# Fewer changes of TensorE tiling: products that take their neighbours' form, reversed keys, merged masks

## The chip, the cores and the metric

The kernel runs on one core of a Trainium2 chip. The metric is device time in microseconds (us); the kernel before takes 242.95 us, the median of three runs (242.12 to 243.84).

A core has five engines that run side by side, each with its own queue of instructions: TensorE (PE, matrix products, with a separate record PEld for the loading of weights), VectorE (DVE), ScalarE (ACT), GpSimd (POOL) and SyncE (SP), which here only issues DMA transfers. They wait for one another through semaphores. TensorE writes to PSUM, eight banks of 512 float32 columns in 128 partitions; VectorE and ScalarE read PSUM and write SBUF; GpSimd works within SBUF.

## The reference, cut to what matters

Two branches over the same 2048 tokens of width 640 are mixed by a gate. Branch A is attention in four segments of 512 tokens, 32 heads of width 20, causal within a segment, with a memory carried from segment to segment. Branch B is a Fourier filter over tokens and width.

```python
def _A_ref(x, wq, wk, wv, wo, beta):
    ...                                   # q, k, v: [B, 32, 4, 512, 20]
    phi = lambda t: jnp.where(t > 0, t + 1.0, jnp.exp(t))
    mask = (ar[:, None] < ar[None, :]) * -1000000000.0
    g = _sigmoid(beta)
    for s in range(4):
        logits = einsum('bhqd,bhkd->bhqk', qs, ks) * scale + mask
        a_dot = einsum('bhqk,bhkd->bhqd', softmax(logits), vs)
        a_mem = einsum('bhld,bhde->bhle', phi(qs), M) / (einsum('bhld,bhd->bhl', phi(qs), z) + 1e-06)
        outs.append(g * a_mem + (1.0 - g) * a_dot)
        M = M + einsum('bhld,bhle->bhde', phi(ks), vs)
        z = z + einsum('bhld->bhd', phi(ks))
    return o @ wo

def _B_ref(x, w_r, w_i):
    X = rfft2(x.astype(float32)) * (w_r + 1j * w_i)
    return irfft2(X, s=(S, D)).astype(bfloat16)

g = _sigmoid((x * gate_w).sum(-1, keepdims=True))
return g * a + (1 - g) * b
```

## The kernel before, in words

The kernel does not issue instructions by hand. `record` lists every operation with its engine (or two engines that may take it), the buffers that it reads and writes, and a priority; `Sched.op` derives from the buffers which operations must come before which. `Sched.schedule` then takes a long list of numbers, `ORDER`, which fixes the sequence of every engine's queue and, where there is a choice, the engine: each number is twice an operation's index plus the choice. `emit` writes the instructions and puts a semaphore wait ahead of an operation where what it needs is not yet known to be done. PSUM banks are handed out from two pools while the list is followed, 0 to 3 for the attention scores (`qk`) and 4 to 7 for all else (`gen`).

**Tiling of TensorE.** A product may use the whole 128x128 array or a part of it. Four forms occur. Whole-array products (mode 0: projections, the Fourier products F1, D, T, Tb, Db, the memory's read and update); products of 128 rows by 32 columns, four beside each other (mode 2: `projd`, `pvf`, `Fb`); products with 20 rows for the scores (mode 1); and 128x64 pairs (mode 4: v tiles of odd token blocks). Mode -1 leaves the form open: `mms` then writes the product either whole or as four 32-wide pieces, by what stands beside it in TensorE's queue. Before, only the output projection of the first three segments (line 513) is of mode -1. The pieces are written at line 513, everything else at line 515.

**Attention.** For each segment `project` makes q and k (five tiles of 128 rows each, five products deep), v (`v_tile`, four blocks of 128 tokens in two halves of 16 heads) and the gate's column, which is a 321st column of the second half's weights (`gw`). The keys of a segment stand in the order of `token_order`: even blocks of 128 first, then the odd blocks, with the two halves of 64 of each odd block exchanged. To match, odd v tiles are made as two products of 64 columns each that land in exchanged partitions. `qk_unit` makes the scores of a group of four heads in three kinds of unit, ScalarE takes the exponential (line 1265) into one of three slots of `ex`, GpSimd zeroes what lies above the diagonal with `affine_select` (line 1286, in `mask`), and `pv_flipped` or, for the last segment, `pv_group` multiplies by v.

**Fourier.** `fold` sums and differences the halves of x (lines 902 and 907, on VectorE or GpSimd), F1 and D transform, T applies the twiddle factors, line 1441 multiplies with the filter W out of PSUM on VectorE, line 1446 combines, Tb and Db transform back, line 1487 sums the halves into G. Copies out of PSUM are lines 524 (ScalarE) and 526 (VectorE).

**End.** `finish_tile` adds, for each 128 tokens, the gated Fourier part (`Fb`) and the output projection in one bank, copies it into `ot` and stores it.

**Queues.** All loads and stores but two go by SyncE's queue, in the list's order; line 547 is a transposing load, line 549 a plain one. At the start its order is an xsb load (x for the Fourier branch), the first transposed chunk of x, beta, the first 192 columns of wk, two transposes of two chunks each, and then the rest of wk; the first columns of wq go by ScalarE's queue. A DMA waits besides until the one that lies 1.6 MB of transfers back has landed.

## Time and profile before

| | before |
|---|---|
| median of three runs, us | 242.95 (242.12 to 243.84) |
| span of the profiled execution, us | 239.9 (the page states no other time of it) |
| TensorE busy, us | 225.7 (94%) |
| weight loads busy, us | 138.7 (58%) |
| VectorE busy, us | 195.9 (82%) |
| ScalarE busy, us | 199.1 (83%) |
| GpSimd busy, us | 165.8 (69%) |
| granted TensorE clock | 1.000 |
| exponentials, line 1265 | 138.7 us busy on ScalarE, 92 instructions |
| masks, line 1286 | 121.3 us busy on GpSimd, 224 instructions |
| odd v tiles, 128x64 products | 160 instructions |

A busy share is an average over stages with different limits. The span runs from the first to the last instruction; the device time has some 3 us besides. Matmuls are pipelined, so that the records of neighbouring products overlap and their mean length says less than the distance from one start to the next. The chain that ended last is followed backwards from the last instruction, at each step to what released it; its shares say which engine set the pace. A wait is idle time of an engine just before an instruction, put down to what came last.

### The profile page before, as it was taken

How to read it: one execution, taken by the hardware profiler on the slowest of the kernel's cores; microseconds unless marked ns; L12 is line 12 of the kernel's file. 1: busy time of each engine (PE TensorE's matmuls, PEld its weight loads, DVE VectorE, ACT ScalarE, POOL GpSimd, SP SyncE). 2: the span in 40 equal slices, each digit the busy share in tenths (PEclk: the TensorE clock that was granted, in tenths of full speed). 3: DMA queues.
4: the chain of work that ended last, by engine and by line, in shares of the span. 5: the costliest groups of instructions: out<-in, count | busy, mean ns of one | idle time of the engine just before them, and what ended most of it. 6: DMA issues, size and time to landing. Idle time of an engine off the chain costs nothing.

```text
span 239.9 us, 9221 instructions
## 1 busy us (share of the span) xinstructions
PE 225.7 (94%) x3837; PEld 138.7 (58%) x3849; DVE 195.9 (82%) x481; ACT 199.1 (83%) x241; POOL 165.8 (69%) x297
## 2 busy tenths in 40 slices
PE   7899999999999999999989999899999998998994
PEld 2475567765456566455646555455544456665793
DVE  0479998889899996898999798997988887855563
ACT  2189688898899999999999979999999987896730
POOL 8514259457969956937974999875899867686820
PEclk9999999999999999999999999999999999999999
DMA  7999869984996795473788672364766698992223
GB/s 157 270 369 234 228 177 182 311 156 112 209 263 161 128 240 170 106 240 76 239 221 251 159 222 65 103 168 138 193 193 187 202 220 127 100 110 80 61 85 109
DMA packets 58924, 42.11 MB, mean 176 GB/s; under 512 B 30020, under 2 KB 55172, under 8 KB 58884
## 3 DMA queue, kind: packets, MB, share of 16 engines
q1 hardware_dynamic: 57844, 40.96, 70.2%
q8 instruction: 30, 0.49, 0.9%
q10 hardware_dynamic: 1040, 0.57, 0.8%
q14 instruction: 10, 0.08, 0.1%
HBM read 23.32 MB, written 12.30 MB: 148 GB/s over the span
## 4 chain that ended last, share of the span: by engine, by line
PE 57%; DVE 17%; ACT 15%; DMA 4%; issue 3%; SPq 2%; POOL 0%; DVEq 0%; ACTq 0%
PE psum L515 51%; ACT ex L1265 10%; PE psum L513 6%; DVE Pt L1441 3%; DMA out_dram<-ot 2%; DMA wk<-in_A_wk_dram 2%; SPq L547 2%; DVE xsb L907 2%; DVE xf L902 2%; ACT et L1073 1%; DVE va L1116 1%; DVE ub L526 1%; DVE phk L1086 1%; DVE q L526 1%; DVE phk L1085 1%
## 5 line engine op out<-in xcount | busy, mean ns | idle before, releaser
L1265 ACT ACTIVATE ex<-psum 128x2048 bf16<-128x2048 f32 (+4 forms) x92 | 138.7, 1507 | 12.6 <-PE psum L515 11.2
L1286 POOL TENSOR_SCALAR_AFFINE_SELECT ex<-ex 128x256 bf16<-128x256 bf16 (+2 forms) x224 | 121.3, 563 | 39.0 <-ACT ex L1265 35.6
L515 PE MATMUL psum<-xT,wk 128*128 128x256 bf16 (+1 forms) x280 | 34.0, 273 | 1.0 <-DMA wk<-in_A_wk_dram 0.8
L515 PE MATMUL psum<-qkp 20*64 20x64 bf16 (+5 forms) x1024 | 31.5, 266 | 3.4 <-ACT ex L1265 2.4
L515 PE MATMUL psum<-wv,xT 128*64 128x320 bf16 (+3 forms) x240 | 30.1, 303 | 0.4 <-DVE va L1116 0.3
L515 PE MATMUL psum<-xT,wq 128*128 128x512 bf16 (+1 forms) x123 | 27.1, 380 | 0.8 <-DMA xT<-in_A_x_dram 0.5
L1441 DVE TENSOR_TENSOR Pt<-psum,Wt 128x642 bf16<-128x642 f32 x32 | 25.6, 822 | 2.3 <-PE psum L515 1.9
L515 PEld LDWEIGHTS psum<-xT,wk 128*128 128x128 bf16 (+1 forms) x280 | 19.9, 97 | 7.5 <-DMA wk<-in_A_wk_dram 1.1
L515 PEld LDWEIGHTS psum<-qkp 20*64 20x64 bf16 (+1 forms) x1024 | 12.2, 100 | 20.4 <-ACT ex L1265 14.4
L513 PE MATMUL psum<-wo,oU 128*32 128x320 bf16 x480 | 21.9, 300 | 0.0
L907 POOL TENSOR_TENSOR xsb<-xf 128x320 bf16<-128x320 bf16 (+2 forms) x12 | 9.4, 787 | 16.6 <-DVE xsb L907 12.4
L515 PEld LDWEIGHTS psum<-wv,xT 128*64 128x64 bf16 (+1 forms) x240 | 14.9, 105 | 7.7 <-issue 2.6
L1116 DVE TENSOR_TENSOR va<-psum,ebx 128x320 bf16<-128x320 f32 x32 | 15.2, 483 | 4.4 <-ACT gate L1114 2.3
L515 PE MATMUL psum<-big,Ac 128*128 128x160 bf16 (+2 forms) x96 | 18.1, 258 | 0.7 <-DVE Pt L1441 0.3
L515 PE MATMUL psum<-big,Cp 128*128 128x321 bf16 (+1 forms) x96 | 18.1, 303 | 0.2 <-DVE G L1487 0.2
L515 PE MATMUL psum<-ex,va 128*32 128x512 bf16 (+4 forms) x480 | 17.3, 275 | 0.9 <-DVE Pt L1441 0.3
L1487 DVE TENSOR_TENSOR G<-eo,psum 128x320 bf16<-128x320 f32 x32 | 14.7, 482 | 3.5 <-PE psum L515 2.5
L526 DVE CAST ot<-psum 128x320 bf16<-128x320 f32 x21 | 10.0, 490 | 8.7 <-PE psum L513 5.3
L515 PE MATMUL psum<-tt,Yt 128*128 128x256 bf16 (+1 forms) x96 | 16.5, 275 | 0.3
L515 PEld LDWEIGHTS psum<-ex,va 128*32 128x32 bf16 x480 | 10.4, 96 | 9.9 <-POOL ex L1286 3.3
L1073 ACT ACTIVATE et<-qu 128x512 bf16<-128x512 bf16 x25 | 15.6, 629 | 0.2
L513 PEld LDWEIGHTS psum<-wo,oU 128*32 128x32 bf16 x480 | 12.0, 96 | 4.6 <-issue 1.2
(99 smaller groups left out, 391.1 us busy)
## 6 DMA issues: line engine op xcount, KB each, us to landing
qkp<-qk_scr SPq DMA_DIRECT2D x28, 160.0 KB
tt<-tab_tt SPq DMA_DIRECT2D x8, 512.0 KB, 3.9
qk_scr<-qu SPq DMA_DIRECT2D x12, 256.0 KB, 3.5
u_scr<-ub SPq DMA_DIRECT2D x12, 256.0 KB, 4.0
xsb<-in_A_x_dram SPq DMA_DIRECT2D x8, 320.0 KB, 6.4
oU<-u_scr SPq DMA_DIRECT2D x15, 128.0 KB, 3.1
out_dram<-ot SPq DMA_DIRECT2D x12, 160.0 KB
Wt<-in_B_w_r_dram SPq DMA_DIRECT2D x16, 80.2 KB, 3.4
```

Of the source, the lines that this page charges most:

```text
L513: h = e.matmul(dst, wt, r_, start=st, stop=sp_, **{**kw, "tile_position": (0, q), "skip_group_check": True})
L515: h = e.matmul(o_, l_, r_, start=st, stop=sp_, **kw)
L526: alts["dve"] = (lambda e: e.tensor_copy(dst(), src()), 67 + 1.04 * n, 68.0)
L547: return e.dma_start_transpose(d_, s_)
L902: self.either(lambda e, r=r, op=op: e.tensor_tensor(xf.ap(r * 642, [321, 2], [1, 320]), xs.ap(o, [D, 2], [1, 320]), xs.ap(o + 320, [D, 2], ...
L907: self.either(lambda e, dst=dst, src=src, d0=d0, n=n, op=op: e.tensor_tensor(xs.ap(o + dst, [D, 2], [1, n]), xf.ap(src + d0, [321, 2], [1, ...
L1073: self.one("act", lambda e: e.activation(et.ap(0, [1, L]), qsl(), ACT.Exp), L, [qb], [b("et", pi_)], late, name="phi_exp")
L1116: self.one("dve", lambda e: e.tensor_tensor(va.ap(i * H * VW + h0 * VW, [VW, nh], [1, DH]), self.ps(bank, 0, [DH, nh], [1, DH]), self.ebx. ...
L1265: self.one("act", lambda e, d=d, q=q: e.activation(self.ex.ap(*d), self.ps(bank, *q), ACT.Exp, scale=SC), n, [bank], [self.exb(s, 2 * pr + ...
L1286: self.one("pool", lambda e: e.affine_select(self.ex.ap(e0 + d0, [1280, 4], [1, n], np_=np_), self.ex.ap(e0 + s0, [1280, 4], [1, n], np_=np_),
L1441: self.one("dve", lambda e, ri=ri, Pt=Pt, Wt=Wt, wo_=wo_, bank=bank: e.tensor_tensor(Pt.ap(ri * 322, [644, 2], [1, KD]), self.ps(bank, 0, ...
L1487: self.one("dve", lambda e, q=q, n2=n2, bank=bank, eo=eo: e.tensor_tensor(self.G.ap(n2 * D + 639 * q, [1 - 2 * q, 320]), eo.ap(q, [1, 320] ...
```

## The change

The change has six parts.

1. All products of mode 0 that belong to the projections, the v tiles, the Fourier branch and the memory become mode -1, so that they may run as four 32-wide pieces where a neighbour does. The 64-wide mode 4 is gone.
2. The keys of odd blocks are now in fully reversed order (step -1 over 128 tokens) in place of exchanged halves. For v, a copy `xR` holds the odd blocks of x reversed; it is made once for each segment on GpSimd or ScalarE, and odd v tiles are plain products with it. The gate's column of odd tiles comes from the unreversed x, by a product with one column.
3. With reversed keys the masks have another shape: two of three become narrower, and the masks of two neighbouring groups of heads may be one instruction (`gs`).
4. Dependencies are kept finer: the two halves of a v tile (`vb`), the two halves of the fold's buffer and its four results (`xsf`, `xs_done`), the parts of the exponentials (b0, b1, b2, c0, c1). Within one engine an order that only comes from reuse of a bank no longer costs a wait (`ordered`), and the waits ahead of one instruction are sorted by when they are expected to end.
5. Banks are no longer handed out from pools but listed (`HOMES`).
6. `ORDER` is a new list, so that every queue has another sequence and other choices of engine: for instance 24 of 32 sums of line 1446 lie on GpSimd instead of 16, and at the start SyncE issues the transposes first, while the first part of wk goes by ScalarE's queue.

```diff
@@ Sched.op
+        for b in w2:
+            if not isinstance(b, Bank):
+                dep(b.w)
+                for q in b.r:
+                    dep(q)
+        o.hard = set(preds)
         for b in w2:
-            bb = b
             if isinstance(b, Bank):
                 o.banks.append(b)
                 b.ops.append(o)
-                bb = b.buf
-            dep(bb.w)
-            for q in bb.r:
-                dep(q)
+                dep(b.buf.w)
...
+    def ordered(p, o):
+
+        return p.eng == o.eng and not p.dma and (p.eng == "pe" or p in o.preds and p.id not in o.hard)
...
@@ emit
-                if p.eng == "pe" and e == "pe":
+                if self.ordered(p, o):
                     continue
...
-                self.Sc.schedule(self.POOLS, self.ORDER)
+                self.Sc.schedule(self.ORDER, self.HOMES)
...
+        self.xR = [T(f"xR{i}", [P, 10 * P], at=(self.tt[0].off, self.tt[1].off, self.on.off, self.on.off + 2560)[i]) for i in range(4)]
...
@@ fold
-                [b("xsb", q)], [b("xf", k)], 1.0, name="fold")
+                [b("xsb", q)], [b("xf", k, r)], 1.0, name="fold")
...
-                [b("xf", k)], [b("xsb", q)], 1.0, name="fold")
+                [b("xf", k, src // 642)], [b("xsf", q, n_)], 1.0, name="fold", after=[b("xsb", q)])
+
+    def xs_done(self):
+
+        return [self.b("xsb", q) for q in range(8)] + [self.b("xsf", q, n_) for q in range(8) for n_ in range(4)]
@@ project
+        xR = self.xR[s]
+        self.Sc.group += 1
+        rev = lambda: (xR.ap(0, [256, 5], [P, 2], [1, P]), xT.ap(2 * P - 1, [L, 5], [256, 2], [-1, P]))
+        self.Sc.op({"pool": (lambda e: e.tensor_copy(*rev()), 1340.0, 50.0), "act": (lambda e: e.activation(*rev(), ACT.Copy), 1130.0, 110.0)},
+                   r=xb, w=[b("xR", s)], prio=t0, name="xrev", after=[b("xf", k, r) for k in range(3) for r in range(2)] if s > 1 else ())
@@ token_order
-        return [(0, 256, lambda: xT.ap(c * L, [256, 2], [1, P])), (256, 256, lambda: xT.ap(c * L + P + 64, [256, 2], [-64, 2], [1, 64]))]
+        return [(0, 256, lambda: xT.ap(c * L, [256, 2], [1, P])), (256, 256, lambda: xT.ap(c * L + 2 * P - 1, [256, 2], [-1, P]))]
@@ proj_tile (the same for memrd, mupd, F1, D, T, Tb, Db)
-            self.mms(items, [b("w" + which + "a"), b("w" + which + "b"), xb[c], bank], [], prio, name="proj", mode=0)
+            self.mms(items, [b("w" + which + "a"), b("w" + which + "b"), xb[c], bank], [], prio, name="proj", mode=-1)
@@ v_part
-            for p0, t0, n in ((0, 64, 64), (64, 0, 64)) if i % 2 else ((0, 0, P),):
...
-            self.mms(items, [b("wv"), xb[c], bank] + ([b("gw")] if h0 else []), [], prio, name="vproj", mode=4 * (i % 2))
+            items = [((lambda c=c: (self.ps(bank, 0, [1, w]), xR.ap(c * 256 + (i // 2) * P, [1, P]) if i % 2 else xT.ap(c * L + i * P, [1, P]),
+                                    self.wv.ap(c * (D + 1) + h0 * DH, [1, w]), c == 0, c == 4, {"skip_group_check": True})), w)]
+            if h0 and i % 2:
+                items.append(((lambda c=c: (self.ps(bank, 320, [1, 1]), xT.ap(c * L + i * P, [1, P]),
+                                            self.wv.ap(c * (D + 1) + D, [1, 1]), False, c == 4, {"skip_group_check": True})), 1))
+            self.mms(items, [b("wv"), xb[c], bank] + ([b("xR", s)] if i % 2 else []) + ([b("gw")] if h0 else []), [], prio, name="vproj", mode=-1)
...
+    def vb(self, s, lts, h0, nh):
+
+        return [self.b("va", s % 2, lt, h) for lt in lts for h in range(2) if h0 < 16 * h + 16 and h0 + nh > 16 * h]
@@ qk_unit (masks)
-                self.mask(s, g, 64, 512, 512, P, (), ("b0", "m1"), prio, -64)
+                self.mask(s, gs, 64, 576, 576, 64, (), ("b0",), prio, -63, 1)
...
-                self.mask(s, g, P, 512, 0, 64, ("a0",), ("m1",), prio, 64)
+                self.mask(s, gs, P, 512, 0, 64, ("a0",), ("m1",), prio, 1 - P, 1)
...
-                self.mask(s, g, 64, 1152, 1152, P, (), ("c0", "m3"), prio, *((0, -512) if s < 3 else (-64, 64)))
+            for gs in (gs,) if self.exo(s, gs[1]) > self.exo(s, gs[0]) else (gs[:1], gs[1:]):
...
+                self.mask(s, gs, 64, o, o, 64, (), ("c1",), prio, -63, 1)
...
@@ mask
-            self.ex.ap(e0 + d0, [1280, 4], [1, n], np_=np_), self.ex.ap(e0 + s0, [1280, 4], [1, n], np_=np_),
-            [[0, 4], [step, n // 64], [1, 64]], ALU.is_ge, 0.0, base=base, channel_multiplier=-1), 4 * n, [self.exb(s, g, k) for k in rk],
+            self.ex.ap(e0 + d0, [1280, n4], [1, n], np_=np_), self.ex.ap(e0 + s0, [1280, n4], [1, n], np_=np_),
+            [[0, n4]] + ([[64, n // 64]] if n > 64 else []) + [[1, 64]], ALU.is_ge, 0.0, base=base, channel_multiplier=cm), n4 * n,
...
@@ fft
-                         2 * P * 2048, [], [b("tt", ti)], early, name="ld_tt")
+                         2 * P * 2048, [], [b("tt", ti)], early, name="ld_tt", after=[b("xR", g // 2)] if g < 4 else ())
```

The first two copies `xR` lie where the twiddle tables `tt` come later, so the first loads of `tt` wait for the odd v tiles of the first two segments.

More of the change, by code (lines that the diff above doesn't have):

```diff
@@ L198, in schedule @@
-        while len(self.order) < len(order):
-            best = None
-            for e in self.eng:
-                t = head(e)
-                if t is not None and (best is None or t < best[0] - 1e-9):
-                    best = (t, e)
-            if best is None:
-                raise RuntimeError("order cannot be kept: " + str([(e, queue[e][pos[e]].name, queue[e][pos[e]].id) for e in self.eng if pos[e] < len(queue[e])]))
-            t, e = best
-            o = queue[e][pos[e]]
-            pos[e] += 1
-            for b in o.first:
-                _, b.pool, b.bank = place(b, level)
-                for q in range(b.bank, b.bank + b.n):
-                    level[b.pool][q] = None
-                    o.dyn.extend(users.get(q, ()))
-            o.t0 = t
+            for b in o.banks:
+                if b.ops[0] is o:
+                    for q in range(b.bank, b.bank + b.n):
+                        assert users[q] is not None
+                        t = max(t, level[q])
+                        o.dyn.extend(users[q])
+                        users[q] = None
@@ L228, in schedule @@
                 free[e] += 43.0
-                gate = window()
-                if gate is not None:
-                    o.dyn.append(gate)
+                tot, i = 0, len(issued) - 1
+                while i >= 0 and tot <= self.WINDOW:
+                    tot += issued[i].nbytes
+                    i -= 1
+                if i >= 0:
+                    o.dyn.append(issued[i])
                 issued.append(o)
@@ L1465, in fft @@
                            r=[bank], w=[b("Cp", g, c0)], prio=prio3, name="ev_Tb",
-                           after=[b("xsb", q) for q in range(8)])
+                           after=self.xs_done())
         cpb = [b("Cp", g, c0) for g in range(16) for c0 in (0, 2)]
```

190 lines of the change are left out of this document (78 added, 112 removed), and 202 rows, old and new, of tables (HOMES, ORDER).

## The prediction

> **What bounds the kernel now.** I read the page's first part, then the chain that ended last, then TensorE's waits, and last its timeline, for the price of a change of tiling.
>
> ```profile
> span 239.9 us, 9221 instructions
> PE 225.7 (94%) x3837; PEld 138.7 (58%) x3849; DVE 195.9 (82%) x481; ACT 199.1 (83%) x241; POOL 165.8 (69%) x297
> PE 57%; DVE 17%; ACT 15%; DMA 4%; issue 3%; SPq 2%; POOL 0%; DVEq 0%; ACTq 0%
> ```
>
> TensorE works 94% of the span and carries 57% of the chain. VectorE and ScalarE carry 17% and 15% of it, GpSimd nothing. In the table by stretch, with TensorE, weight load, VectorE, ScalarE and GpSimd busy in that order after the length,
>
> ```profile
> 60.00:180.00 120.00, 115.03 (x1706) 66.22 (x1715) 108.71 (x269) 113.45 (x125) 94.01 (x177) 1.00 0.68 177
> ```
>
> ScalarE stands close behind TensorE: 113.45 of 120 us. So TensorE sets the time, and ScalarE is the next to be late. The view of TensorE's own waits is short; its list sums to some 9 us, led by
>
> ```profile
> PE psum L515 <- ACT ex L1265: 2.4, 9, 0.4
> PE psum L515 <- ACT ot L524: 1.5, 2, 0.9
> PE psum L515 <- DVE G L798: 1.3, 1, 1.3
> PE psum L515 <- DMA wk<-in_A_wk_dram: 0.8, 2, 0.6
> ```
>
> Busy time hides a second loss. TensorE's timeline (start, length, then the products) shows it by its starts:
>
> ```profile
> 60.15 0.38 PE L515 MATMUL psum<-xT,wq 128*128 128x512 bf16 x1
> 60.36 0.23 PE L515 MATMUL psum<-big,Ac 128*128 128x161 bf16 x1
> 60.43 0.38 PE L515 MATMUL psum<-xT,wq 128*128 128x512 bf16 x1
> 60.74 0.73 PE L515 MATMUL psum<-ex,va 128*32 128x512 bf16 x20
> ...
> 231.01 2.40 PE L515 MATMUL psum<-wo,oTl 128*32 128x320 bf16 x64
> 233.23 0.31 PE L515 MATMUL psum<-G,fbg 128*32 128x320 bf16 x4
> ```
>
> A 512-column product is followed after 0.21 us by another whole-array one (60.15 to 60.36), but after 0.31 us by a 128x32 one (60.43 to 60.74): 0.10 us for the change of tiling. Over all such pairs of starts the middle excess over the columns is 96 ns from whole to 32 wide, 109 back, 96 from whole to the 20-row form, 106 back, 101 from the 64-wide form to whole. I count 232 changes in the old order of instructions: **23.7 us** of the span.
>
> **The change, part by part.**
>
> *Tiling.* In the new order of instructions I count 171 changes instead of 232. Per direction at the prices above this is 17.7 us, so **-6.0**. Thirty of the old changes touch the 64-wide form, which is gone; the others fall away where a product runs in its neighbour's form. They fall over the four segments of the sequence as 11, 19, 15 and 15 fewer.
> What a split costs: four 128x32 pieces stand for one whole product (TensorE instructions 3849 to 4926). The 64 pieces from 231.01 are 16 sets of 320 columns and take 2.22 us, 139 ns a set; 320 columns at the 0.21 us per 512 of a whole product are 131 ns. Over all neighbours of one form the middle is 136 ns for both. I take nothing; with 374 sets newly split and 8 ns for each, the upper end is +3.0.
> [...] The trace does not show a loss: 32-wide loads take 96 ns each, whole ones 97, and both hide. [...]
>
> *Columns.* Over the two orders, columns times their rate (1/2.4 ns, as 512 in 0.213 us) are 179.8 and 179.3 us: **-0.5**, from the products whose keys come 64 wide.
>
> *Gate column.* Odd v tiles take their operand from xR, which is reversed, so the gate's column needs its own product with one column from xT: 40, of which 5 sets are split. The nearest row is the 21-column product, 25 ns from start to start (40 in 1.0 us from 227.89 to the change before 228.98): **+1.0**. Below nothing is excluded, since work is only added; the upper end is a load each, 96 ns, +3.8.
>
> *Reversed keys.* The k projection reads its second half with step -1. No product of before has such an operand. A gain is excluded, since it reads the same elements. The lower end is 0: VectorE's fold reads one operand backwards and takes 353 ns for 320 columns, a forward sum of 321 takes 365; GpSimd's fold takes 758 against 732. The upper end is half rate: 100 whole products of 256 columns and 10 sets, 107 ns more each, +11.8. I take 0, from the rows with the same step.
>
> *The copy xR.* Four of 128x1280. Two are on ScalarE, whose 1280-element activation takes 1.24 us; two on GpSimd, between 1.1 us (its memset's 0.87 ns per element) and 2.8 (its two-input sum, 1402 ns per 640). The first stands in ScalarE's queue before the first exponential, which waited 0.93 us for TensorE at 13.7; so 0.3 us may show, and behind it wait beta's exponential and all of ScalarE. I leave it in the range. The copy on GpSimd is hidden by its 31% of idle time. Odd v tiles wait for xR; if that cover fails, the products behind one wait up to 2.8 us.
>
> *Masks.* Per row: 128 of 478 ns, 64 of 670, 32 of 691 become 126 of 478, 33 of 670 to 691, 32 of 691: 124.3 to 105 us. Not on the chain (POOL 0%), so nothing by itself. It pays for what moves to GpSimd: eight W sums (732 each), two gate tables (1157), three sums into oU, two copies; some +12 us. GpSimd nets -7.
>
> *ScalarE.* Off: 8 gate exponentials (165), 6 of Cp (602, 368), 3 of Bt (538), 1 ub, 2 oTl; on: 2 xR, 4 ot (435), 2 Ac (602), 2 q (600). Net -0.8, but the 60 to 180 us stretch loses some 5.9, since the added ones lie at the ends. VectorE, by the same count, nets -3.6. So the stretch that TensorE shortens by some 3.5 us asks of ScalarE 107.5 of 116.5 us: it is not late.
>
> *Waits.* Evictions of halves, folds and v tiles get keys of their own, and waits within one engine on a bank fall away. VectorE sets the chain from 18 to 36 us, but TensorE has other work there: 19.55 of 20 us between 20 and 40. I cost this at nothing.
>
> *Head.* The chain's first long piece (start, length):
>
> ```profile
> 6.95 4.92 DMA wk<-in_A_wk_dram
> 12.00 6.32 PE psum L515 x68
> ```
>
> The rest of wk is issued at 6.95, behind an xsb load, beta, the first part of wk and three transposes. In the new order the three transposes come first, one xsb load after them, and the first part of wk goes by ScalarE's queue. Transposes take SP 1.23, 1.61 and 1.61 us, the xsb issue 0.4: 0.78 + 4.9 = 5.7 us, so wk's rest starts and lands 1.2 us earlier: **-1.2**. It lasts only if the evictions between (three on ScalarE) follow; lower end of the gain 0, upper 1.5. The folds start later for it, and their cover is the 2 to 4 us which GpSimd sat idle between them.
>
> **Sum.** -6.0 - 0.5 + 1.0 - 1.2 = **-6.7 us**, the waits of some 9 us unchanged: span 233.2. The page gives a span of 239.9 and no other time for that execution; the runs' median is 242.95, 3.05 more, which I carry over. **236.2 us**, 2.8% faster.
>
> **Rivals.**
> 1. *The waits fall too* (14%). GpSimd, ScalarE and VectorE are all relieved, and most of TensorE's waits are for them. Half of 9 us gone: 231.7. Against it: the order is rewritten everywhere, and each wait is its own.
> 2. *ScalarE takes the place* (9%). If the exponentials set the pace between 40 and 200 us, the 5.1 us of changes saved in the last three segments turn into waits of the score products: 241.4. For it: ScalarE at 19.52 of 20 us between 100 and 120, and 15% of the chain. Against it: its evictions in that stretch go to VectorE.
> 3. *The order does not fit the chip* (6%). Every queue and bank is fixed by it; if its costs miss, TensorE's waits double, and the gain becomes +2.3: 245.2. For it: GpSimd's idle time shows it is easily waited for; against it: the old list is fixed in the same manner and leaves 9 us.
> 4. *Slower by the reversed read* (5%). At half rate the 110 reads cost 11.8: 236.2 + 11.8 = 248.0. It decides from 57% of that price on, where it takes the gain of 6.7. For it: nothing in the trace excludes it for TensorE. Against it: VectorE and GpSimd read backwards at no cost.
> 5. *Loads show* (2%). One unhidden 96 ns load in each of the 374 new sets is 36 us: 272. The 139 ns per set with four loads each speaks against it. [...]
>
> **Chances.** The forecast has 64%, with an own range of 233.5 to 239 by the ends of the split, gate and head. Faster by over 1% (about what a measurement of this kernel can tell from no change: below 240.5) are the forecast and rival 1: 78%. Within 1% are rival 2 and half of 3: 12%. Slower are the rest: 10%. The range takes in most of rival 1 and all of rival 2: 230.8 to 243.0.
>
> **What would show it.** Right: 171 gaps of 0.10 us at changes of tiling; split sets of 320 columns at 136 to 139 ns; reversed 256-column products at 109 ns from start to start, as the forward ones; the rest of wk landing near 10.7; ScalarE below 19.5 of 20 us in the middle stretches; TensorE's waits near 9 us. Wrong: reversed products at over 150 ns, TensorE's waits on the exponentials or masks well above 9 us, or an odd v tile that waits for xR by microseconds.

## The result

The changed kernel is slower: 253.56 us, median of 4 runs (248.13 to 256.18), beside 242.53 for the old one (four runs, 242.12 to 243.84), a ratio of 1.028, interval 1.020 to 1.036. The forecast was 236.2 with a range up to 243.0, and its sign was wrong. (Medians hold all runs of a kernel; ratios leave out those over 1.5% above its fastest, here the two above 255 us.)

The profiled execution is the fastest of the four, 248.13 us, at a granted clock of 0.999 (its record begins at 10.1 us; what lies ahead of that is told under "Putting the pieces together"). The page of the changed kernel (span; busy time, share and instructions of each engine; the chain by engine):

```profile
span 246.3 us, 11384 instructions
PE 223.4 (91%) x4926; PEld 145.0 (59%) x4926; DVE 193.4 (79%) x475; ACT 197.5 (80%) x231; POOL 149.9 (61%) x276
PE 40%; DVE 15%; DMA 14%; ACT 12%; SPq 8%; POOL 5%; issue 3%; DVEq 0%; ACTq 0%; POOLq 0%
```

The span grew by 6.4 us while TensorE is busy for 2.3 us less. ScalarE, VectorE and GpSimd all have less to do, and the chain no longer runs mainly along TensorE: DMA has 14% of it. The line by stretch of the changed kernel, columns as before:

```profile
60.00:180.00 120.00, 109.42 (x2532) 68.19 (x2529) 109.10 (x255) 106.65 (x112) 84.44 (x165) 1.00 0.65 170
```

TensorE is busy for 109.4 of 120 us, where it was 115.0, and ScalarE is down by 6.8. So no other engine took TensorE's place; TensorE waits more. The list of its waits that the prediction summed to some 9 us now comes to some 17. The view of its waits (us in total, times, longest):

```profile
PE psum L473 <- ACT ex L1247: 3.0, 10, 0.5
PE psum L471 <- DVE Pt L1429: 1.7, 1, 1.7
PE psum L473 <- DVE va L1095: 1.4, 1, 1.4
PE psum L471 <- DVE va L1095: 1.3, 1, 1.3
...
PE psum L473 <- DMA tt<-tab_tt: 1.2, 1, 1.2
PE psum L471 <- DVE eo L484: 1.0, 1, 1.0
PE psum L471 <- ACT qu L482: 1.0, 1, 1.0
```

Once its start was past, the old kernel had no single wait over 0.9 us; here the six lines shown below the first are one wait each, of 1.0 to 1.7 us.

Busy time hides part of it, so I split the span by TensorE's starts. From one product's start to the next, the columns at 1/2.4 ns (512 in 0.21 us) are work, a change of tiling is 105 ns (96 to 109 by direction in the old profile), and what is left counts as a wait where it is over some 40 ns (and as work where less). The tail is what follows TensorE's last product.

```
kernel                          changes  work  changes' time  waits  tail   span  clock
old                                 232  191.4      24.4       19.1   3.5   239.9  1.00
changed                             171  195.3      18.0       26.7   4.7   246.3  1.00
changed, profiled again             171  194.2      18.0       34.1   5.0   252.8  0.96
changed, products whole             214  192.1      22.5       22.1   3.7   241.9  1.00
old order, split form opened        214  192.7      22.5       24.6   4.4   245.7  1.00
old order, whole change             195  194.2      20.5       30.5   3.2   249.9  0.99
old order, whole change, whole      215  192.0      22.6       26.9   3.9   246.9  1.00
```

(Another 1.6 us of each lie ahead of the first product and in the last. In profiles with stretches at half clock, the slower products can swell both work and waits: in the head of the changed kernel a split set of 256 columns takes 215 ns before the full clock is there and 110 after.) Each row is one execution. The changes of tiling gave about what was forecast, 6.4 us at 105 ns each. Against it stand 3.9 us of work (products at half clock in the head are part of it), 7.6 of waits and 1.2 of tail.

### The profile page after: what moved, and what is told of

Its sections match the earlier page's. It is cut to its first block, busy times and chain, and to the rows that moved or that the text cites. A ratio compares the mean times of both kernels' runs of the same rounds, so it can differ in the third digit from the quotient of the medians.

```text
span 246.3 us, 11384 instructions
## 1 busy us (share of the span) xinstructions
PE 223.4 (91%) x4926; PEld 145.0 (59%) x4926; DVE 193.4 (79%) x475; ACT 197.5 (80%) x231; POOL 149.9 (61%) x276
## 4 chain that ended last, share of the span: by engine, by line
PE 40%; DVE 15%; DMA 14%; ACT 12%; SPq 8%; POOL 5%; issue 3%; DVEq 0%; ACTq 0%; POOLq 0%
PE psum L473 25%; PE psum L471 15%; ACT ex L1247 11%; SPq L505 5%; SPq L507 4%; POOL ex L1273 4%; DMA fcat<-tab_fcat 3%; DMA tt<-tab_tt 2%; DMA pkn<-phk 2%; DVE Pt L1429 2%; DMA qk_scr<-qu 2%; DMA xsb<-in_A_x_dram 2%; DMA u_scr<-ub 2%; DVE phq L1064 2%; DVE Cp L484 2%
## 5 line engine op out<-in xcount | busy, mean ns | idle before, releaser
L1247 ACT ACTIVATE ex<-psum 128x2048 bf16<-128x2048 f32 (+4 forms) x92 | 137.2, 1505 | 17.6 <-PE psum L473 13.9
L1273 POOL TENSOR_SCALAR_AFFINE_SELECT ex<-ex 128x256 bf16<-128x256 bf16 (+3 forms) x191 | 93.8, 514 | 32.2 <-ACT ex L1247 27.7
L1434 POOL TENSOR_TENSOR Yt<-Pt 128x321 bf16<-128x321 bf16 x24 | 17.5, 736 | 15.5 <-DVE Pt L1429 11.9
L473 PE MATMUL psum<-xT,wk 128*128 128x256 bf16 (+1 forms) x220 | 22.4, 293 | 0.8 <-DMA xT<-in_A_x_dram 0.8
L877 POOL TENSOR_TENSOR xsb<-xf 128x318 bf16<-128x318 bf16 (+2 forms) x9 | 7.0, 793 | 20.7 <-DVE xf L872 20.7
L473 PE MATMUL psum<-ex,va 128*32 128x192 bf16 (+4 forms) x480 | 17.7, 273 | 0.8 <-DVE Cp L484 0.3
L473 PE MATMUL psum<-xT,wq 128*128 128x512 bf16 (+1 forms) x95 | 18.0, 419 | 0.0
L473 PEld LDWEIGHTS psum<-ex,va 128*32 128x32 bf16 x480 | 11.8, 96 | 7.7 <-issue 1.4
L473 PE MATMUL psum<-wv,xT 128*128 128x320 bf16 (+2 forms) x90 | 15.3, 248 | 0.0
L484 DVE CAST Cp<-psum 65x256 bf16<-65x256 f32 (+1 forms) x26 | 13.6, 536 | 1.6 <-PE psum L471 1.2
L872 DVE TENSOR_TENSOR xf<-xsb 128x640 bf16<-128x640 bf16 x16 | 7.3, 482 | 8.1 <-DMA xsb<-in_A_x_dram 8.1
L471 PE MATMUL psum<-xT,wq 128*32 128x512 bf16 x160 | 11.6, 380 | 2.3 <-DVE va L1095 1.3
## 6 DMA issues: line engine op xcount, KB each, us to landing
oU<-u_scr SPq DMA_DIRECT2D x15, 128.0 KB, 3.8
```

Of the source, the lines that this page charges most:

```text
L471: h = e.matmul(dst, wt, r_, start=st, stop=sp_, **{**kw, "tile_position": (0, q), "skip_group_check": True})
L473: h = e.matmul(o_, l_, r_, start=st, stop=sp_, **kw)
L484: alts["dve"] = (lambda e: e.tensor_copy(dst(), src()), 67 + 1.04 * n, 68.0)
L1247: self.one("act", lambda e, d=d, q=q: e.activation(self.ex.ap(*d), self.ps(bank, *q), ACT.Exp, scale=SC), n, [bank], [self.exb(s, 2 * pr + ...
L1273: self.one("pool", lambda e: e.affine_select(self.ex.ap(e0 + d0, [1280, n4], [1, n], np_=np_), self.ex.ap(e0 + s0, [1280, n4], [1, n], np_ ...
L1434: fn = lambda e, r=r, a0=a0, a1=a1, op=op, Pt=Pt, Yt=Yt: e.tensor_tensor(Yt.ap(r * 322, [1, KD]), Pt.ap(a0 * 322, [1, KD]), Pt.ap(a1 * 322 ...
```

## Experiments

### Is it the order, or the split form?

Four kernels on one chip. First the changed kernel again, unaltered.

> The changed kernel, unaltered, to see which of its losses come back. Theory A (the new order does not fit: its products, reads and masks cost what was forecast, but transfers land later and VectorE is held by GpSimd longer than the order allows for): 248 to 252 us again, with the gap of TensorE before a Tb product near 125 us and those behind odd v tiles near 47 and 148 us in the same places, each over 1 us. Theory B (TensorE's form 128x32 itself costs, by a lower granted clock): the time again, with a granted clock below 0.99 and products at more than 139 ns per 320 columns in some stretch. If the waits fall in other places, neither holds as put.

255.58 us, median of 4 (252.54 to 258.48), beside 243.92 for the old kernel. The granted clock of these runs is 0.962 to 0.980, and it was 0.999, 0.979, 0.966 and 0.973 in the first four. In 42 runs of the old kernel on these chips it is 0.996 on average, and under 0.99 in three. So the loss has two parts: some 6 us at full clock, and more that goes with a lower clock. The spans of the eight runs are 246.3 us at 0.999, 250.2 at 0.98 (mean of two) and 254.6 at 0.966 (mean of five).

Second, the old kernel with only the split form opened, in its own order (the first pair of lines likewise for memrd, mupd, F1, D, T, Tb and Db):

```diff
-  ... name="proj", mode=0)
+  ... name="proj", mode=-1)
-  ... name="vproj", mode=4 * (i % 2))
+  ... name="vproj", mode=4 if i % 2 else -1)
```

> The kernel before, with its old order, in which only the form of whole-array products is left open (v tiles of odd blocks stay 64 wide). Changes of tiling 232 to 212, instructions 3849 to 4951. Theory A: the split is free, and the 20 changes bring at most 1.8 us: 241 to 243 us, waits where they were. Theory B: the split products lower the clock or hold TensorE; 245 us or more, with a clock below 0.99.

250.82 us (247.57 to 252.39), ratio 1.022, interval 1.011 to 1.033, at clocks of 0.986 to 1.0. Eighteen changes fewer, and yet slower. TensorE's waits in this kernel begin with a line that the old one hardly has (0.3 us there):

```profile
PE psum L513 <- issue: 3.1, 5, 1.3
PE psum L515 <- ACT ex L1265: 2.3, 10, 0.3
...
PE psum L515 <- issue: 0.7, 3, 0.4
```

"issue" means that TensorE stood still and nothing in the profile released it. L513 is the helper's line for split pieces. By starts these gaps sum to 5.9 us; in the old kernel 2.2. The loss is clear, but its size is not: the interval reaches from 1% to 3%.

Third, the whole change in the old kernel's order, engines and banks; fourth, the changed kernel in its new order with every product of the split group run whole (`mode=-1` back to `0`).

> The whole change but its list: copy xR, reversed keys, narrower masks, finer dependencies and open tiling, in the sequence, engines and banks of the kernel before (new operations set in just ahead of their first use, a merged mask at its first part's place). Changes of tiling 193. Theory A: -3.7 for the changes of tiling, -0.5 columns, +1.2 for 40 one-column products at 29 ns: 239.5 to 241 us. Theory B, or a cost in the copy or the reversed keys: 246 us or more, as with the new list.

254.67 us (251.67 to 256.65), ratio 1.044, interval 1.033 to 1.054: the second theory's time. The split form and the new data flow come together here, so this run alone does not tell them apart; the same kernel with its products whole follows further down.

> The changed kernel with its new list, where all products that the change leaves open run whole again (the output projection of the first three segments stays open). Changes of tiling 171 to 214, 4.1 us more of them. Theory A: slower than the changed kernel by what of the 4.1 us does not fall into its waits, 0 to 4 us. Theory B: faster than the changed kernel, 243 us or less, with the clock back at 1.0.

248.11 us (243.73 to 248.72). All four runs are faster than every run of the unaltered changed kernel beside them, although there are 43 changes of tiling more. At full clock it is 241.9 against 246.3 us: 4.5 us given back in changes, and 3.2 of work, 4.6 of waits and 1.0 of tail taken off. So the order alone is not the cause. But the expected 243 us at a clock of 1.0 came in one run only: the other three have clocks of 0.972 to 0.983 and spans of 246.1 to 246.9, so the lower clock stays without the split form. By these pairs of single profiles the split form costs about twice what it saves in the new order, and in the old one (7.7 us of work, waits and tail against 1.9) four times.

### Why the split form costs in the old order: TensorE's instructions

The timeline of TensorE in the old order with the split form opened, at one of the gaps (start, length, products, in brackets the idle time):

```profile
18.57 0.29 PE L513 MATMUL psum<-fcat,xsb 128*32 128x128 bf16 x8
18.68 0.39 PE L513 MATMUL psum<-xT,wk 128*32 128x256 bf16 x8
20.34 0.84 PE L513 MATMUL psum<-xT,wk 128*32 128x256 bf16 x24 [1.27 <-issue]
```

It stands between two products of the same kind. The page counts the DMA packets that bring instructions; of the old kernel, and of this one:

```profile
q8 instruction: 30, 0.49, 0.9%
```

```profile
q8 instruction: 39, 0.64, 1.1%
```

Each packet has 16,384 bytes. The program of TensorE has two instructions a product (its weight load and itself) and 94 others, 9,996 in all: over 39 packets 256 a packet. I counted TensorE's instructions up to each gap over 0.25 us with the name "issue": 448, 705, 5045, 5301, 7088 and 8368. Modulo 256 that is 192, 193, 181, 181, 176 and 176 (8 products are missing in the trace, which lowers the later counts by up to 16). And each gap ends 1.26 to 1.48 us after a packet has landed. That looks as if TensorE waited for its next 256 instructions. A split set of 256 columns uses 8 instructions in 109 ns, a whole product 2; at that rate 256 instructions last some 3.5 us.

Two experiments on that. In one the k projections stay whole, which takes the runs at 14.6 and 18.8 us away:

```diff
-  ... name="proj", mode=-1)
+  ... name="proj", mode=-1 if which == "q" else 0)
```

> The old kernel with the split form open to all whole-array products but the k projections (4544 products instead of 4951; 214 changes of tiling instead of 212 by the order). Theory 1, instruction supply: TensorE's instructions arrive in packets of 16,384 bytes, 256 instructions each, and a run of split products of few columns (8 instructions in 109 ns) empties what is there before the next packet has landed. Then the gaps at 14.6 and 18.8 us of the earlier kernel (0.92 and 1.42 us, inside the split k projections) are gone, gaps that nothing in the profile explains sum to 2.5 to 4 us instead of 5.9, and those left move to other products, since 640 to 800 instructions fewer shift every packet's border, but stay at 176 to 193 modulo 256 in TensorE's count of instructions and end 1.0 to 1.6 us after a packet. TensorE's last product ends near 238.5 to 239.5 us (241.3 before), the span is 242 to 243.5. Theory 2, the split form costs for another reason (its weight loads, the DMA load of the moment): the gaps near 135, 139, 186 and 213 us stay at the same products, and their position in the count of instructions is no longer the same modulo 256.

247.72 us (246.15 to 249.61), ratio 1.017, interval 1.010 to 1.025. The median is 3 us below that with all split, but the ratios, each to the old kernel beside it, are 1.017 and 1.022 and their intervals overlap: a gain in time is not shown. Both gaps are gone, as expected; the unexplained ones sum to 2.3 us, and the two over 0.25 us lie at 184 and 177 modulo 256, in other products. The profiled span, 246.8, misses the expected 242 to 243.5: at 201 to 210 us waits for ScalarE and VectorE of 1.5, 1.0 and 0.7 us appear, followed by two stretches at half clock. Its best run, at full clock, has a span of 244.1 and misses it too.

The other only shifts the packets' borders. All is split as before, but the warm-up at the head is cut finer:

```diff
-  10 x one product of 512 columns
+  10 x eight products of 64 columns
```

> The old kernel with the split form open to all whole-array products, as in the run with gaps at 14.6, 18.8, 135, 139, 186 and 213 us; only each of the ten warm-up products of 512 columns is issued as eight of 64 columns, which puts 140 instructions more ahead of all the rest and changes nothing behind them. Instruction supply: no unexplained gap over 0.25 us stays at a product where it was; those that come lie at 170 to 195 modulo 256 in TensorE's count of instructions, that is at 30 to 55 in the old count, so that they fall between other products (70 products earlier, or 58 later). If instead the split products or their operands make the gaps, they stay at the same products, and lie at 60 to 80 modulo 256 in the new count.

255.68 us (254.83 and 256.53), ratio 1.046, interval 1.035 to 1.057. No gap stayed where it was. Six new ones came, 1.15 to 2.15 us each, at 704, 960, 5057, 7873, 8129 and 8384 instructions (no product is missing in this trace): 192, 192, 193, 193, 193 and 192 modulo 256. They end 1.23 to 1.59 us after a packet. Its waits:

```profile
PE psum L513 <- issue: 4.4, 3, 2.0
PE psum L515 <- issue: 3.5, 3, 1.3
PE psum L515 <- ACT ex L1265: 2.2, 9, 0.3
```

That settles it for the old order: behind the warm-up, the same products in the same order lose 4.4 or 8.9 us in gaps over 0.25 us, by where the borders of 256 fall. In these twelve gaps TensorE goes on 1.2 to 1.6 us after the landing of a packet. That it waits there for the instructions of the packet is my inference; the profile names no releaser.

In the changed kernel itself this is the smaller part: 1.0 us in its first profile (at 193 modulo 256 and, which does not fit, at 65), 2.2 in its second, of which one gap of 1.93 us lies at 179. Nor does it need split products. The changed kernel with its products whole has such a gap too, at 209.8 us:

```profile
PE psum L473 <- issue: 0.7, 1, 0.7
```

It ends 1.49 us after a packet, some 4 us behind a run of 76 products of 21 columns, which start some 25 ns apart. So the packets do not explain why the whole form is faster in the new order.

### Why the clock falls

In the second profile of the changed kernel the clock drops in the middle of the span. The table by stretch (length, the engines' busy time in the order of the page, granted clock, DMA share, GB/s):

```profile
124.60:128.00 3.40, 1.65 (x39) 1.01 (x32) 3.40 (x7) 2.07 (x3) 1.79 (x3) 1.00 0.63 172
128.00:131.40 3.40, 3.40 (x30) 2.12 (x29) 3.08 (x10) 2.54 (x3) 1.71 (x4) 0.50 0.01 4
131.40:134.80 3.40, 3.29 (x94) 2.09 (x92) 3.05 (x9) 2.74 (x3) 1.91 (x3) 1.00 0.34 54
196.20:199.70 3.50, 2.46 (x72) 1.41 (x60) 2.39 (x6) 2.73 (x5) 0.24 (x1) 0.99 0.78 213
199.70:206.50 6.80, 6.16 (x112) 3.16 (x116) 3.63 (x10) 3.13 (x5) 5.52 (x10) 0.50 0.83 145
```

TensorE was busy for 1.65 of 3.4 us, with one wait of 1.9 us in it; the next 3.4 us run at half clock. The record of the clock has steps of 3.41 us throughout (in the profiles of the old and the changed kernel the stretch at full clock lasts 235.52 us, 69 of them). So a wait may be paid twice. To test this on a kernel with neither split products nor a new order, I put three pauses into the old one, by cutting three of VectorE's products into 41 pieces:

```diff
+  step = 8 if g in (3, 7, 11) and ri == 1 else KD
-  W_mul: one tensor_tensor over KD columns
+  W_mul: one tensor_tensor for each step columns
```

> The old kernel, with VectorE's second multiplication into Pt of three frequency groups (near 75, 110 and 140 us) cut into 41 pieces of 8 columns; the result is the same. An estimate from the shortest VectorE operations of its trace (some 65 to 75 ns each): 2.7 to 3.1 us instead of 0.82, so TensorE gets three pauses of up to some 2 us. Theory 1, a pause costs twice, since a stretch of 3.4 us in which TensorE is busy for less than some 0.6 is followed by one at half clock: at least one of the pauses is followed by a stretch at half clock in the profile, the mean clock over the runs is 0.975 to 0.99 (1.0 or 0.99 in most runs of the old kernel), and the span is 246 to 250. Theory 2, the lower clock of the changed kernel comes from the split products or the chip's state and not from its waits: no stretch at half clock, mean clock as in the old kernel's runs beside it, span 242 to 246 from the pauses alone.

255.73 us (255.08 to 257.94), ratio 1.050, interval 1.044 to 1.056. The clock is 0.973, 0.973, 0.973 and 0.958. Its table:

```profile
77.70:81.10 3.40, 2.01 (x36) 1.14 (x37) 3.37 (x25) 0.92 (x3) 2.96 (x7) 1.00 0.28 78
81.10:84.50 3.40, 3.40 (x14) 1.57 (x12) 2.06 (x6) 2.03 (x2) 0.83 (x2) 0.50 0.65 147
...
115.20:118.60 3.40, 1.26 (x33) 0.72 (x33) 3.40 (x20) 1.82 (x5) 2.07 (x6) 1.00 0.00 0
118.60:125.40 6.80, 4.98 (x38) 3.46 (x42) 5.16 (x12) 2.75 (x3) 4.48 (x7) 0.50 0.81 227
...
149.30:152.80 3.50, 1.03 (x7) 0.34 (x6) 3.50 (x37) 2.21 (x3) 1.52 (x4) 0.99 0.72 214
152.80:156.20 3.40, 3.40 (x54) 1.76 (x54) 2.56 (x7) 0.88 (x1) 1.66 (x4) 0.51 0.50 152
```

Each pause is followed by half clock. TensorE stood still for 2.0, 1.9, 2.6 and 2.6 us, 9.1 in all (the pieces took 80 ns each, so the pauses were longer than I had estimated, and so was the loss); 13.6 us at half clock can cost up to 6.8 more, an estimate from the 215 and 110 ns a set in the changed kernel's head. The span is 13.9 longer. So waits of some 2 us can lower the clock; the split form isn't needed for it.

Over the profiles of all these kernels, between head and tail, I cut the span into such steps. All nine in which TensorE was busy for 0.51 or less were followed by half clock (two of them ran at half clock themselves); of 21 between 0.52 and 0.63, eight were; of 19 between 0.64 and 0.75, one. The old kernel's lowest is 0.74. Where the borders of the steps fall is part of it: the wait of 1.75 us ahead of the same product lies whole in one step of the changed kernel's second profile (124.6 to 128.0 us, busy share 0.49, half clock follows), and in the first profile it is cut by a border at 126.1 us (shares of 0.76 and 0.66, no half clock). What else decides I can't say, and two stretches at half clock (one in the changed kernel's second profile, at 213 us, and one at 207 us in the kernel `whole_port_warm` below) have a busy step ahead of them. In the changed kernel's first profile the lowest is 0.57, and half clock did not follow; its span is the shortest of the eight runs.

### Where the changed order waits

The longest wait, at 125 to 127 us, in the changed kernel's timeline (VectorE, GpSimd and TensorE):

```profile
123.91 1.16 POOL L1273 TENSOR_SCALAR_AFFINE_SELECT ex<-ex 128x256 bf16<-128x256 bf16 x3 [0.52 <-ACT ex L1247]
...
124.56 1.86 DVE L1064 TENSOR_SCALAR phq<-qu 128x512 bf16<-128x512 bf16 x1
...
125.02 1.24 POOL L924 COPY xR<-xT 128x1280 bf16<-128x1280 bf16 x1
126.34 0.24 DVE L1139 RECIPROCAL dn<-dn 128x16 f32<-128x16 f32 x1
126.50 0.76 DVE L1429 TENSOR_TENSOR Pt<-psum,Wt 128x642 bf16<-128x642 f32 x1
...
127.31 0.40 PE L471 MATMUL psum<-tt,Yt 128*32 128x256 bf16 x6 [1.75 <-DVE Pt L1429]
```

This step of `phq` takes 0.28 us as a rule. Here it takes 1.86, and ends 0.15 us after an unbroken run of GpSimd's: three masks and the copy xR. Pt comes late by that, and TensorE waits 1.75 us. At 146.4 us the second step of another `phq`, 0.42 us as a rule, takes 2.69 us beside two sums, a product and a mask of GpSimd's without a gap, and ends 0.33 us after that mask, inside the next one. Both come back at the same places in the second profile and in the kernel with its products whole (where TensorE waits 1.7 us for Pt again), so they belong to the new order and data flow and not to the split form. The longest of the same operations in the old kernel is 0.88. So I took those GpSimd operations away: the copies xR of the last two segments go to ScalarE, the two sums to VectorE.

```diff
 ORDER   # twice the operation's number, plus one for its second engine
-  2782, ... 3418, ... 1373, ... 1375      # xR, xR on GpSimd; Yt, Yt on GpSimd
+  2783, ... 3419, ... 1372, ... 1374      # xR, xR on ScalarE; Yt, Yt on VectorE
```

> The changed kernel, but the xR copies of segments 2 and 3 run on ScalarE instead of GpSimd and the two Yt sums near 146 us on VectorE instead of GpSimd. Theory 1, VectorE's operations are stretched while GpSimd runs these (phq took 1860 ns at 124.6 us and 2692 ns at 146.4 us, 226 and 360 ns at best): both fall below 1000 ns, TensorE's stalls of 1.90 us before the Tb products at 125 us and 1.50 us ahead of the projection at 148 us fall below 0.6 each, the sum of stalls from 26.7 (34.1 in the second profile of the changed kernel) to 22 to 24.5 us at full clock, and the span at full clock is 243 to 244.5. Theory 2, the order sets these waits (the operand would be late anyway): the stalls stay over 1.2 us each, the span is 245 to 248 at full clock.

Taking the copy away takes the long `phq` away. At the same place, in this kernel:

```profile
128.47 0.28 DVE L1064 TENSOR_SCALAR phq<-qu 128x512 bf16<-128x512 bf16 x1
```

No `phq` takes more than 0.75 us, and both waits fall below 0.4. Three masks without a gap run beside this one too (127.83 to 129.03 us), and do not hold it. In the changed kernel 16 of 60 steps of `phq` and `phk` lie wholly beside GpSimd's work, and only these two take over 0.9 us. So an unbroken run of GpSimd's stands beside each long one, but is not enough; what else it takes is open. But the kernel gains nothing: 253.80 us (251.0 to 254.96), ratio 1.038, interval 1.030 to 1.047. ScalarE's copy of 1.26 us now stands ahead of `qu`, for which TensorE waits 1.2 us at 130.5, and ahead of Cp, 0.8 at 95.2; the loads that it waits for (va behind a transpose at 47 us, tt at 83) take 2.1 and 1.8 us; and three gaps at packet borders (178 to 181 modulo 256) come to 3.1 us, one of 1.4 at 141.6. Two more without a releaser, of some 0.5 us each, do not fit: they end 3.6 and 4.4 us after a packet. Three of its steps of 3.41 us have a busy share of 0.42 to 0.59, and each is followed by half clock. The expected 22 to 24.5 us of waits were 33.4.

Does the change cost anything without the split form and without the new order?

> The whole change (reversed keys, the xR copies, merged masks, one-column gate products) in the old kernel's order, engines and banks, with every whole-array product run whole (215 changes of tiling by the order; 232 in the old kernel). It takes the split form away from the run in the old order (249.9 us span, stalls of 30.5). Theory 1, the changed data flow by itself costs little: stalls of 19 to 21 us, span 239 to 241 (old kernel 239.9: 1.7 us less for changes of tiling, 1.0 more for the gate's column, up to 1 for xR ahead of the first exponential). Theory 2, the data flow costs (odd v tiles wait for xR, merged masks come later, xR slows VectorE): stalls of 23 us or more, span 243 or more. Against the new order with whole products (241.9 us): if this one is the faster, the searched order itself loses on the chip.

249.10 us (248.48 to 256.02), ratio 1.022, interval 1.016 to 1.028, and a span of 246.9 at full clock: the second theory's side. Of its 7.8 us more in waits, 6.9 are for VectorE, and its two longest waits, 1.64 us each, follow a `phk` of 2.37 us and a `phq` of 1.83 beside runs of masks and sums on GpSimd. It is also 5.0 us longer than the new order with products whole (241.9), so the new list is the better of the two for this data flow. It is no verdict on the data flow, though: the merged masks' places in the old order were chosen by me, and another choice might leave gaps between them.

### Putting the pieces together

The last two kernels keep the new order, run all products whole, move xR and the sums off GpSimd, and do all ten warm-up products ahead of the first projections (the new order had put two of them behind eight pieces of projections):

```diff
-  14, 16, 190, 18, 46, 20, 34        # 18 and 20: the last two warm-up products; 190, 46: projections
+  14, 16, 18, 20, 190, 46, 34
```

> The changed kernel's order with every whole-array product run whole (as in the run of 241.9 us), the same moves off GpSimd as in the other kernel of this batch, and all ten warm-up products ahead of the first projections. If the interrupted warm-up is what left the clock at half until 10.1 us, the full clock is granted by 5 to 7 us and the first products with the rest of wk start at 11.9 to 12.3 us instead of 13.2. With both theories right the span is 237.5 to 239.5 us at full clock, which would beat the old kernel's 239.9; with only the warm-up right 240.5 to 241. [...]

245.00 us (241.62 to 248.61, 10 runs), ratio 1.000, interval 0.995 to 1.004: level with the old kernel. The expected 237.5 to 239.5 us at full clock was missed; the one run at 1.000 has a span of 241.0, which is what was put down for the warm-up alone. The full clock is there at 6.1 us, where it was at 10.1, and the first products with the rest of wk start earlier. In the changed kernel's first profile, and in this one:

```profile
5.68 0.62 PE L473 MATMUL psum<-xT,wk 128*32 128x256 bf16 x8 [0.78 <-DMA xT<-in_A_x_dram]
...
13.21 0.61 PE L473 MATMUL psum<-xT,wk 128*128 128x256 bf16 x4
```

```profile
11.17 1.05 PE L473 MATMUL psum<-xT,wk 128*128 128x256 bf16 x8 [0.26 <-DMA wk<-in_A_wk_dram]
```

An interrupted warm-up does not always cost this. In the changed kernel's second profile, with the same interruption, the full clock is there at 5.1 us and these products start at 11.54; in the three other profiles with it, the first among them, the full clock comes at 9.6 to 10.2. In the nine with the warm-up in one piece it comes at 4.2 to 7.1.

Instead TensorE waits 1.5 us at 47.8 for a va that stands behind a `phk`, which sits for a transpose, and 1.2 us for `qu` behind ScalarE's xR. In the last kernel that `phk` stands behind the va, and only the inverse products of 321 columns may be split (10 changes fewer):

```diff
-  1960, ... 2130                       # phk ahead of va
+  ... 2130, 1960
-  ... name="Db", mode=0)
+  ... name="Db", mode=-1)
```

> The changed kernel's order with whole products, the moves off GpSimd and the warm-up as in the run of 243.5 us, and two edits: only the inverse products big,Cp (321 columns) may take the split form (202 changes of tiling instead of 212 by the order), and in VectorE's order one phk near 48 us, which sat 2.03 us for a transpose with two va behind it, stands behind the va that TensorE waited 1.70 us for. If long split products in short runs cost nothing and the waits were set by the place of phk, stalls fall from 23.3 to 21 to 22 us and the span at full clock is 238.5 to 240.5, the median 241.5 to 244. If the split form costs even here, or the wait moves on to the next operation, the median stays at 245.

246.61 us (243.76 to 251.22, 12 runs), ratio 1.011, interval 1.007 to 1.015: not the expected 241.5 to 244, but the case where the wait moves on. The wait at 47.8 is gone. But TensorE waits 2.0 us for the score operands' load at 37.8, 1.2 for `qu` at 127 and 1.3 for `eo` at 196, and behind each of these a step at half clock follows. No version beat the old kernel.

## Why the prediction was wrong

Two steps turned the sign: the waits, put at nothing, grew by 7.6 us, and the split form, put at nothing too, costs 8.8 us of work, waits and tail by the kernel without it, 4.6 of them in those waits. Even at its upper end, +3.0, the split term alone would have left the forecast at 239.2. By its own steps, in the profile at full clock (span 233.2 forecast, 246.3 measured):

- *Tiling, -6.0.* Right: 171 changes, 96 to 110 ns each by direction in the middle, but for whole to 20-row, where 122 includes waits.
- *A split costs nothing, upper end +3.0.* This step failed. In size first: with the same order, the split form takes 3.2 us more of work than whole products, for 372 sets 8.6 ns each, so the upper end was about the value (one pair of profiles; in the old order 1.3 us, 3.5 ns each). The middle over neighbours, 136 and 109 ns, is the same for both forms and hid it; the long tail of a few late sets is only in the mean. And in kind: the step priced the set by itself, and neither its instructions nor what it does to the waits. That 3849 products become 4926 was written there and given no cost; in the old order it shows as gaps at packet borders.
- *Loads (rival 5).* It fell: weight loads of 32 columns take 97 ns in the middle, whole ones 98, and no load shows per set: the 8.6 ns above are less than a tenth of one.
- *Columns, gate column.* Right within what can be read: a one-column product takes 29 ns, against 25.
- *Reversed keys, 0 (rival 4, +11.8).* Right: 109 ns for 256 columns backwards, whole and split, as forwards.
- *xR, "hidden by GpSimd's 31% of idle time".* Wrong. The danger was not that an odd v tile waits for the copy; it was what VectorE does beside it (`phq` in 1.86 us). One wait of 1.75 us at 125 us goes with the copy, and is gone where it is moved; on ScalarE it stands before `qu` and costs 1.2.
- *Masks and what moves to GpSimd, 0.* GpSimd has 16 us less to do (7 forecast), and still VectorE operations beside it take up to 2.69 us at two places where its operations follow each other without gaps.
- *Head, -1.2.* Measured +1.2: 13.21 us instead of 12.00. The rest of wk was issued at 5.78 us as forecast, but took 5.6 us and landed at 11.4, 0.5 earlier than before; and the projections from 5.7 to 10.1 us ran at half clock. Where they did not, it is -0.5 (second profile) and -0.8 (warm-up in one piece).
- *Waits unchanged, 0.* This step failed by most. Measured +7.6. 3.0 of it come with the order and the data flow (products whole), 4.6 more with the split form. Rival 3, waits doubled, was nearest, and had 6%; its reason, that the order does not fit, covers only the 3.0.
- *The clock.* No step had it. All rows of the old profile show 1.00, and I took that as given. The run with pauses shows that it goes with the old kernel's short waits (0.958 to 0.973 with the pauses in); the changed kernel's median, some 6 us above its run at 0.999, goes with clocks of 0.962 to 0.980.
- *The range.* The ends of the split, the gate and the head term, +3.0, +2.8 and +1.2, add up to 243.2, and not to the 239 given as the forecast's own upper end. The tail, +1.2, is in no term.

What stays open: why in the new order the split form lengthens waits for va, tt, `qu` and oU, 4.6 us in all, when gaps at packet borders are some 1 us there with split and with whole products; what besides an unbroken run of GpSimd's makes a VectorE operation long; and what the data flow costs in an order made for it without split products.

## What to carry to other kernels

Splitting a product into column tiles multiplies instructions (here 3849 products became 4926); look at how many instructions a microsecond TensorE needs in the densest run, because in runs at some 70 (8 in 109 ns) TensorE here stood still at packet borders (4.4 us in gaps over 0.25 us in one kernel), and a warm-up cut finer, which shifts the code by 140 instructions, left one kernel some 5 us slower in the median. A wait of TensorE of some 2 us within 3.4 can cost more than its length, since half clock may follow: 9.1 us of standstill made the old kernel's span 13.9 longer. Read the clock's row of the old profile as a result of its short waits and not as a constant: 1.00 there, 0.958 to 0.973 with three pauses put in. Where VectorE and GpSimd work side by side, look for long VectorE operations beside unbroken runs on GpSimd: here one of 0.28 us took 1.86.

## What the runs showed of the hardware

- Gaps of TensorE at the same place in blocks of 256 instructions: 12 of 12 over 0.25 us without a releaser, in two kernels, lie at 176 to 193 in its count and end 1.2 to 1.6 us after the landing of a 16,384-byte packet. In the other profiles four of 0.3 to 0.6 us do not fit. The prediction says nothing of that queue: in the old order with the split form opened it moves 0.64 MB and takes 1.1% of the DMA engines.
- Half clock in steps of 3.41 us after stretches in which TensorE is busy for about half: always (nine times) at 0.51 or less, eight times of 21 at 0.52 to 0.63. In the old kernel with pauses, gaps of 1.9 to 2.6 us did it.
- A VectorE operation that takes 0.28 us as a rule took 1.86, and one of 0.42 took 2.69, beside unbroken runs of GpSimd; they ended 0.15 and 0.33 us after the end of a GpSimd instruction. Most others beside such work took their usual time.
